# Range tests of five units moved to the end, small copies and weight casts moved to ScalarE, new engine orders

## The chip, the cores and the metric

One core of one Trainium2 chip runs the whole kernel. The metric is the device time of one execution in microseconds (us); the kernel before takes 573.07 us, the median of three runs (572.95 to 573.48).

## The reference, cut to what matters

A gated linear attention with a complex decay runs first; its output goes through one dense layer pair with a Mish-like gate.

```python
# attention: q, k, v, a_re, a_im are (4, 8, 768, 48)
scale = np.minimum(mag, 0.999) / (mag + 1e-06)         # mag = |a|
S_re, S_im = new_re + kv, new_im                       # new = a_n * S, per step t
y[:, :, t] = np.einsum('bhd,bhde->bhe', q[:, :, t], S_re)
# dense part: x is (3072, 384), w_in (384, 2048), w_out (2048, 384)
h = x @ w_in
g = h * np.tanh(np.log1p(np.exp(h)))
out = g @ w_out
```

The inputs of the dense weights arrive as 64-bit words and are turned into fp32 and then into pairs of fp32r parts on the chip.

## The kernel before

**Tiling.** The 3072 tokens are 12 units of 256 (four batches of three units), each of two chunks of 128. A unit passes three stages. `ew_steps(u)` turns the decay into magnitudes and phases (VectorE and ScalarE, tiles of 128 x 768; units 0 and 1 do it in two groups, g0 and g1, of 128 x 384), and ends with four rotations `rot` on VectorE whose results SyncE copies ("relays") into the transposed tile T by small DMAs. `attn_steps(u)` does the attention of two chunks on TensorE (score tile `pa`, transposed keys `pkn`, output `ypsum`, state update `pd`), with masks and state sums on VectorE and copies out of PSUM on ScalarE; its result goes by four DMAs into `xf`, is split into `xH` (ScalarE) and `xL` (VectorE, L258), and these feed the dense part. `moe_steps` has 8 steps a unit: `mm1` (18 matmuls into `ph`, L697, waiting for xH and xL), four ScalarE passes and two VectorE passes over 128 x 512, a split of g into `gh` and `gl`, and `mm2` (12 matmuls into `po`, L734). The first four steps of units 0 and 1 use unsplit weights (L693 and L730).

**The lines that the change touches.** In `test(g)` (L387) VectorE compares R - 0.55 with a quarter of I squared, which `size(g)` left in x3, and sums the result into `good`; the total over `good` decides at the end, behind everything, whether the general path has to run. `grow(g)` ends with two copies of 128 x 6 (L454, L455), on VectorE for units 0 and 1 and on GpSimd for the others. `divide(n)` (L257, L258) casts 16 weight tiles of 128 x 768 and takes the rest: 11 casts on ScalarE, 5 (n = 2, 5, 8, 11, 14) on VectorE. The cast `gh` of steps 1, 3, 5 and 7 is on ScalarE from unit 2 on. `spin` (L522) issues "junk" matmuls of 128 x 512 that compute nothing the output uses: 40 after the first phase (`turned`) and 44 after the first `ypsum` copy.

**What sets the order.** Every step has a place in the plan, in units of dense steps, and a program emits the plan in that order. But the order in which each engine runs its instructions is written out: `ORDER` has a list of instruction numbers per engine (a number is the place at which the plan emits the instruction on that engine, "20+4" stands for 20 to 23), and `in_order` chains the instructions to it. So each of PE, DVE (VectorE), ACT (ScalarE), Pool and SP runs its own list strictly from front to back, and a waiting instruction holds all behind it. SP issues all DMAs.

Of the kernel before, what the change touches and what calls it, by code (L numbers as in the profile page):

```python
# [14 lines left out]
F32 = mybir.dt.float32  # L15
# [12 lines left out]
P = 128  # L28
# [5 lines left out]
NJ = 3  # L34
# [5 lines left out]
HACT, HMOD = 2, 3  # L40
# [8 lines left out]
WREP, WREP2, WK = 40, 44, -9.4  # L49
# [6 lines left out]
KU = 3  # L56
PU = 3
# [64 lines left out]
    """,  # L122
    "DVE": """
# [96 lines left out]
def tile_kernel(ctx, tc, q, k, v, are, aim, w_in, w_out, out):  # L220
# [83 lines left out]
    good = const.tile([P, UNITS + GRP, 3], F32, name="good")  # L304
    ncar = const.tile([P, NJ], F32, name="ncar")
    units = {}

    def ew_steps(u):
        b, uu = divmod(u, NU)
        st = units[u] = {}  # L310
# [681 lines left out]
```

## Time and profile before

| what | value |
|---|---|
| median of three runs | 573.07 us |
| the profiled execution, its time | 572.9 us |
| its span, first to last instruction | 571.2 us |
| TensorE matmul busy | 546.9 us, 96% |
| VectorE busy | 482.8 us, 85% |
| ScalarE busy | 465.0 us, 81% |
| mean granted TensorE clock | 0.995 of full speed |

1.7 us of the profiled time lie outside its span. A row of instructions names line, engine, operation, the tiles out<-in and the shapes; times are us from the start of the span, and a bracket tells how long the engine had been idle and what ended that. A busy TensorE is modelled: matmuls overlap, and the end of one is an estimate. Starts are exact.

### The profile page before, as it was taken

How to read it: one execution, taken by the hardware profiler on the slowest of the kernel's cores; microseconds unless marked ns; L12 is line 12 of the kernel's file. 1: busy time of each engine (PE TensorE's matmuls, PEld its weight loads, DVE VectorE, ACT ScalarE, POOL GpSimd, SP SyncE). 2: the span in 40 equal slices, each digit the busy share in tenths (PEclk: the TensorE clock that was granted, in tenths of full speed). 3: DMA queues.
4: the chain of work that ended last, by engine and by line, in shares of the span. 5: the costliest groups of instructions: out<-in, count | busy, mean ns of one | idle time of the engine just before them, and what ended most of it. 6: DMA issues, size and time to landing. Idle time of an engine off the chain costs nothing.

```text
span 571.2 us, 13311 instructions
## 1 busy us (share of the span) xinstructions
PE 546.9 (96%) x5254; PEld 509.5 (89%) x5254; DVE 482.8 (85%) x865; ACT 465.0 (81%) x749; POOL 39.5 (7%) x55
## 2 busy tenths in 40 slices
PE   0799999999999999999999999999999999999996
PEld 0367877889999999999999999999999999999996
DVE  6999999999999998988988998888897887554543
ACT  7899898999979899798898989679978777446662
POOL 2022322240000000000000000000000000000000
PEclk9899999999999999999999999999999999999999
DMA  8666966805455747606547437316436326201000
GB/s 298 223 200 219 297 204 184 259 16 152 155 151 143 220 127 198 163 16 182 143 143 202 132 91 224 112 43 203 135 93 173 107 75 157 91 22 36 1 29 32
DMA packets 69059, 80.69 MB, mean 141 GB/s; under 512 B 6144, under 2 KB 60672, under 8 KB 68992
## 3 DMA queue, kind: packets, MB, share of 16 engines
q1 hardware_dynamic: 68992, 79.80, 47.2%
q8 instruction: 42, 0.69, 0.5%
q14 instruction: 25, 0.20, 0.1%
HBM read 44.63 MB, written 11.40 MB: 98 GB/s over the span
## 4 chain that ended last, share of the span: by engine, by line
PE 81%; ACT 8%; DVE 6%; DMA 2%; issue 1%; SPq 1%; ACTq 0%; DVEq 0%
PE ph L697 32%; PE po L734 32%; PE ypsum L610 6%; PE pa L583 5%; PE pd L630 2%; PE po L730 2%; ACT L249 2%; DMA T<-QK 1%; PE ph L693 1%; DVE raw L289 1%; ACT R L488 1%; DVE wx L288 1%; PE junk L522 1%; DVE X L425 1%; ACT X L375 1%
## 5 line engine op out<-in xcount | busy, mean ns | idle before, releaser
L697 PE MATMUL ph<-xH,w 128*128 128x256 f32 x1104 | 223.7, 286 | 0.2 <-ACT X L377 0.2
L734 PE MATMUL po<-w,gh 128*128 128x384 f32 x704 | 201.9, 339 | 0.0
L697 PEld LDWEIGHTS ph<-xH,w 128*128 128x128 f32 x1104 | 180.3, 190 | 2.3 <-issue 0.9
L697 PE MATMUL ph<-xL,w 128*128 128x256 f32 x552 | 156.3, 284 | 0.0
L734 PEld LDWEIGHTS po<-w,gh 128*128 128x128 f32 x704 | 128.8, 188 | 2.2 <-issue 1.3
L734 PE MATMUL po<-w,gl 128*128 128x384 f32 x352 | 118.4, 337 | 0.0
L697 PEld LDWEIGHTS ph<-xL,w 128*128 128x128 f32 x552 | 104.7, 190 | 1.2 <-issue 0.8
L701 ACT ACTIVATE e<-ph 128x512 f32<-128x512 f32 (+1 forms) x100 | 57.0, 573 | 43.0 <-PE ph L697 35.5
L707 DVE SCALAR_TENSOR_TENSOR g<-e,ph 128x512 f32<-128x512 f32 (+1 forms) x100 | 65.7, 658 | 20.0 <-ACT e L705 17.2
L703 ACT ACTIVATE e<-e 128x512 f32<-128x512 f32 (+1 forms) x100 | 60.7, 610 | 22.0 <-DVE e L702 21.8
L734 PEld LDWEIGHTS po<-w,gl 128*128 128x128 f32 x352 | 66.2, 188 | 0.2
L702 DVE TENSOR_SCALAR e<-e 128x512 f32<-128x512 f32 (+1 forms) x100 | 40.7, 408 | 27.1 <-ACT e L701 26.9
L258 DVE TENSOR_TENSOR gl<-g,gh 128x512 fp32r<-128x512 f32 x88 | 60.0, 683 | 2.9 <-ACT gh L257 2.5
L705 ACT ACTIVATE e<-e 128x512 f32<-128x512 f32 (+1 forms) x100 | 60.9, 609 | 1.3
L704 ACT ACTIVATE e<-e 128x512 f32<-128x512 f32 (+1 forms) x100 | 60.6, 609 | 1.3
L249 ACT ACT_TABLE_LOAD x43 | 55.2, 1283 | 1.5 <-PEq L948 0.8
L610 PE MATMUL ypsum<-am,V 128*48 128x128 f32 x240 | 36.1, 278 | 0.6 <-DVE am L597 0.6
L522 PE MATMUL junk<-cmask 128*128 128x512 bf16 x84 | 23.1, 419 | 14.1 <-DVE I L431 14.1
L257 ACT CAST gh<-g 128x512 fp32r<-128x512 f32 x40 | 24.5, 612 | 11.9 <-PE po L734 11.1
L291 POOL TENSOR_TENSOR raw<-raw 128x768 int32<-128x768 int32 x16 | 27.4, 1719 | 86.0 <-DVE raw L289 39.3
L610 PE MATMUL ypsum<-T,S 96*48 96x128 f32 x320 | 32.2, 277 | 0.0
L522 PEld LDWEIGHTS <-cmask 128*128 128x128 bf16 x84 | 8.6, 106 | 23.8 <-issue 17.5
(96 smaller groups left out, 841.7 us busy)
## 6 DMA issues: line engine op xcount, KB each, us to landing
T<-X SPq DMA_DIRECT2D x72, 129.0 KB, 2.5
T<-QK SPq DMA_DIRECT2D x72, 129.0 KB, 2.5
raw<-w_in SPq DMA_DIRECT2D x8, 768.0 KB, 7.2
raw<-w_out SPq DMA_DIRECT2D x8, 768.0 KB, 6.9
kd<-vx SPq DMA_DIRECT2D x45, 128.0 KB, 3.0
kn<-kd SPq DMA_DIRECT2D x15, 384.0 KB, 3.7
V<-v SPq DMA_DIRECT2D x12, 384.0 KB, 4.5
out_dram<-o SPq DMA_DIRECT2D x24, 192.0 KB, 2.4
```

What stands on the lines that cost most here:

```text
L249: nc.scalar.preload_act_table_set({"l": "natural_log_exp_and_others", "t": "trig_and_small"}[name])
L258: leng(out=lo, in0=src, in1=h.bitcast(F32), op=ALU.subtract)
L522: ins = nc.tensor.matmul(junk, cmask, cmask.unsqueeze(1).broadcast_to([P, 4, P]), start=True, stop=True)
L610: nc.tensor.matmul(py[64 * par:64 * par + D, i, :], lhs, rhs, start=n == 0, stop=first or n == 1)
L697: nc.tensor.matmul(ph[:, a, :], rows_in(parts[j][:, wp], kt, a), st[xp][:, kt, :], start=n == 0, stop=n == 8)
L701: act(e, ph, AF.Exp)
L702: nc.vector.tensor_scalar_min(e, e, math.exp(20.0))
L703: act(e, e, AF.Square, bias=1.0)
L704: act(e, e, AF.Ln, scale=0.2, bias=0.2)
L705: act(e, e, AF.Exp, scale=-1.0)
L707: nc.vector.scalar_tensor_tensor(g, e, 2.5, ph, ALU.subtract, ALU.mult)
L734: nc.tensor.matmul(po[t], gp[:, a, tsl], rows_out(parts[NPAIR + j][:, wp], a), start=j in starts and a == 0 and n == 0, stop=j + 1 in ends ...
```

## The change

It does four things.

1. `test` of units 0 to 4 (seven VectorE instructions, two each for units 0 and 1) is left out of its old place. `late_steps(u)` loads R and I of these units a second time (ten DMAs of 384 KB, into the same rotating buffers "R" and "I", two each), squares I on ScalarE (five instructions of 128 x 768) and does the seven tests, at places 82 to 89 of the plan's 96.
2. The two small copies of `grow` for units 0 and 1 (eight instructions) go from VectorE to ScalarE.
3. The five weight casts that were on VectorE go to ScalarE (HACT 3), and so do the casts `gh` of unit 1's steps 5 and 7.
4. 50 instead of 40 junk matmuls in the first `spin`, and new lists for all engines.

```diff
-HACT, HMOD = 2, 3
+HACT, HMOD = 3, 3
-WREP, WREP2, WK = 40, 44, -9.4
+WREP, WREP2, WK = 50, 44, -9.4
+LATER, LATE0, LATED = 5, 82, 1.5
...
+    def in_range(out, R, I2, n):
+        nc.vector.scalar_tensor_tensor(out, R, LOW, I2, ALU.subtract, ALU.is_ge, accum_out=good[:, n, 0:1])
+
+    def late_steps(u):
+        st = {}
+
+        def load():
+            for n, src in (("R", are), ("I", aim)):
+                st[n] = io.tile([P, NCH, NJ, C], F32, tag=n, name=n, bufs=RB)
+                nc.sync.dma_start(st[n].rearrange("p c j t -> p (c j) t"), src[u].rearrange("p (a t) -> p a t", t=C))
+
+        def check():
+            R, I = (st[n].rearrange("p c j t -> p c (j t)") for n in "RI")
+            act(I, I, AF.Square, scale=0.5)
+            if u < GRP:
+                for g in range(NCH):
+                    in_range(I[:, g], R[:, g], I[:, g], UNITS + u if g else u)
+            else:
+                in_range(I, R, I, u)
...
-            nc.vector.scalar_tensor_tensor(x3, R, LOW, x3, ALU.subtract, ALU.is_ge, accum_out=good[:, gi(g), 0:1])
+            if u >= LATER:
+                in_range(x3, R, x3, gi(g))
...
-            small = nc.vector if u < 2 else nc.gpsimd
-            small.tensor_copy(QK[..., C:], X[..., C - 1:C])
-            small.tensor_copy(X[..., C:], X[..., C - 1:C])
+            small = nc.scalar.copy if u < 2 else nc.gpsimd.tensor_copy
+            small(QK[..., C:], X[..., C - 1:C])
+            small(X[..., C:], X[..., C - 1:C])
...
-                split(g, gh, gl, nc.scalar.copy if 1 < unit < UNITS and j in GA else nc.vector.tensor_copy, nc.vector.tensor_tensor)
+                split(g, gh, gl, nc.scalar.copy if 0 < unit < UNITS and j in GA else nc.vector.tensor_copy, nc.vector.tensor_tensor)
...
+    for u in range(LATER):
+        load, check = late_steps(u)
+        plan.append((LATE0 + u * LATED, len(plan), load, LATE0 + u * LATED))
+        plan.append((LATE0 + u * LATED + 1, len(plan), check, LATE0 + u * LATED + 1))
```

The lists are long; read against the plan, their fronts say this (first before, then after).

```diff
 "PE"
-        0+20 48+4 40+4 52+4 20+2 56+4 44+4 60+15 22+13 124+4 75+5 128+2 35 132+4 130 188+6 36+2 226+3 38 80+5 136+4 85
+        0+23 58+4 23+5 62+4 50+7 66+8 57 28+21 74+16 134+8 90+5 198+6 95+16 236+6 142+8 111+6 258 150+32 259+5 117 49
 "SP"
-        0+3 8 3 16 5 4 9 17 11 15 18 7 6 20 19 21+3 46 10 12 24 26+2 25 28+2 45 43+2 42 47 13+2 48 51 31 30 35 33+2 32
+        0+2 6 2 8 3 5 4 7 16 9 17 11 15 18 20+2 23 22 19 10 12 46 26 25 24 27 29 28 47 44 42 45 43 14 13 48 51 31+2 30
```

- **SP.** Before, q and k of unit 0's second group (6 and 7) are loaded behind the first relay (18), and five of the six relays of the first group follow them. After, q (6) is the third DMA of all and k (7) the ninth; the six relays (18, 20, 21, 23, 22, 19) follow each other.
- **PE.** Before, 20 junk matmuls stand ahead of the first score tile (48) and 64 between it and the first `mm1` of unit 1 (L697). After, 23 stand ahead of it, 68 between it and that `mm1`, 3 behind; and one more `mm2` step of unit 0 (two instructions of L730, four rows of the trace) stands ahead of it.
- **DVE.** The last rotation of unit 0's first group is number 22 of the list before and 20 after, with the running sum over the phases of the second group now ahead of it; that of unit 0's second group is number 43 and 36, that of unit 1's second group 87 and 74, `xL` of unit 1 131 and 117.
- **ACT.** The arc tangent of unit 0's second group joins that of the first between the same two table loads. Of the instructions ahead of unit 1's `xH`, the eight small copies and one weight cast are new there.
- From the fourth `mm2` of unit 2 on for PE, and from some place in units 3 and 4 on for DVE, ACT and SP, the lists before and after name the same instructions in the same order, but for the late steps. Those lie between the dense steps of unit 10: the late loads behind the last relay of unit 11 on SP (six of them) and behind unit 11's `xf` (four), the squares and tests between the passes of unit 10's steps.

## Rows read from the trace of the kernel before

**Rows 1.** The page: busy time, and TensorE's busy tenths in 40 slices.
```profile
PE 546.9 (96%) x5254; PEld 509.5 (89%) x5254; DVE 482.8 (85%) x865; ACT 465.0 (81%) x749; POOL 39.5 (7%) x55
...
PE   0799999999999999999999999999999999999996
```
**Rows 2.** Busy us by stretch: stretch, length, engines (instructions), PEclk, DMA share, GB/s.
```profile
24.31:30.34 6.03, 5.48 (x35) 4.10 (x35) 5.98 (x14) 4.55 (x9) 0.00 (x0) 0.72 0.88 319
30.34:52.90 22.56, 21.80 (x210) 15.89 (x211) 22.42 (x43) 21.89 (x38) 5.26 (x3) 1.00 0.66 198
52.90:80.80 27.90, 27.82 (x271) 22.23 (x270) 27.86 (x50) 24.69 (x49) 7.51 (x5) 1.00 0.82 253
80.80:136.20 55.40, 55.40 (x416) 47.11 (x415) 54.68 (x84) 51.22 (x81) 17.05 (x12) 1.00 0.49 156
136.20:189.00 52.80, 52.60 (x525) 50.99 (x524) 52.23 (x94) 46.70 (x72) 0.89 (x5) 1.00 0.57 160
...
500.00:525.00 25.00, 25.00 (x242) 24.29 (x234) 13.53 (x28) 13.95 (x25) 0.00 (x0) 1.00 0.12 33
```
**Rows 3.** The same view, the junk matmuls (L522) alone: PE, PEld, PEclk, DMA.
```profile
24.31:80.52 56.21, 15.91 (x64) 6.21 (x64) 0.97 0.76 238
```
**Rows 4.** The chain that ended last, merged: start, us, what.
```profile
75.04 1.35 PE po L730 x4
...
79.36 1.51 PE junk L522 x7
80.87 2.37 PE ph L697 x18
```
**Rows 5.** Timeline at unit 1's entry into the dense part: start, us, instruction.
```profile
79.92 0.96 DVE L258 TENSOR_TENSOR xL<-xf,xH 128x768 fp32r<-128x768 f32 x1
...
80.52 0.47 PE L697 MATMUL ph<-xH,w 128*128 128x256 f32 x1
```
**Rows 6.** Timeline of the first relays and scores, and of unit 1's last rotation.
```profile
16.53 0.55 DVE L387 SCALAR_TENSOR_TENSOR X<-R,X 128x384 f32<-128x384 f32 x1
17.01 0.95 DVE L472 TENSOR_TENSOR QK<-QK,R 128x768 f32<-128x768 f32 x1
19.91 1.84 SPq L468 DMA_DIRECT2D T<-QK  x3
24.31 1.13 PE L595 MATMUL pa<-T 96*128 96x128 f32 x8 [3.40 <-DMA T<-QK]
...
52.05 0.95 DVE L472 TENSOR_TENSOR QK<-QK,R 128x768 f32<-128x768 f32 x1
```
**Rows 7.** First 200 us by form: instruction, count | busy us, mean ns | idle before.
```profile
L387 DVE SCALAR_TENSOR_TENSOR X<-R,X 128x768 f32<-128x768 f32 x4 | 3.8, 948 | 0.0
L257 DVE CAST w<-raw 128x768 fp32r<-128x768 f32 x5 | 2.8, 554 | 0.0
L387 DVE SCALAR_TENSOR_TENSOR X<-R,X 128x384 f32<-128x384 f32 x4 | 2.2, 555 | 0.0
L455 DVE COPY X<-X 128x6 f32<-128x6 f32 x4 | 0.7, 166 | 0.0
...
L257 ACT CAST w<-raw 128x768 fp32r<-128x768 f32 x11 | 10.0, 911 | 0.9 <-DVE w L258 0.8
L552 ACT COPY kn<-pkn 128x384 f32<-128x384 f32 x10 | 4.6, 468 | 1.1 <-PE pkn L551 1.0
L377 ACT ACTIVATE X<-I 128x768 f32<-128x768 f32 x4 | 3.4, 840 | 0.0
L257 ACT CAST gh<-g 128x512 fp32r<-128x512 f32 x4 | 2.5, 616 | 0.8 <-DVE g L707 0.8
L374 ACT ACTIVATION_READ_ACCUMULATOR X<-R 128x1 f32 x6 | 1.1, 190 | 0.0
```
**Rows 8.** DMA issues between 2.33 and 2.6 us: KB, us to landing.
```profile
raw<-w_in SPq DMA_DIRECT2D x1, 768.0 KB, 5.5
```
**Rows 9.** Who waited for whom, ACT from 80.8 to 136.2: total us, times, longest.
```profile
ACT e L703 <- DVE e L702: 2.0, 5, 0.6
```

More of the change, by code (lines that the diff above doesn't have):

```diff
@@ L75 @@
     "PE": """
[46 rows of a table removed]
[46 rows of a table added]
     """,
     "DVE": """
[29 rows of a table removed]
[29 rows of a table added]
     """,
     "Activation": """
[24 rows of a table removed]
[25 rows of a table added]
     """,
     "Pool": """
-        8 3+2 1 5 10 0 7 9 6 2 11 13 12 14+3 18 17 20 19 21+6 29 28 27 31 30 35 33 32 36 34 38 37 40 39 51 41+2 44 43
-        45+2 48 47 49+2
+        8 3+2 1 5 10 0 7 9 6 2 11+6 18 17 20+2 19 22+5 28+5 27 35 34 36 33 38 37 40 39 51 41+2 44 43 45+2 48 47 49+2
     """,
     "SP": """
[13 rows of a table removed]
[13 rows of a table added]
     """,
@@ L306, in tile_kernel @@
     units = {}
+    def in_range(out, R, I2, n):
[14 more added lines that the diff above has]
+                in_range(I, R, I, u)
+        return load, check
     def ew_steps(u):
```

221 rows, old and new, of the table ORDER are left out of this document.

## The prediction

> **What bounds the kernel now.** I read the page first: TensorE is busy for 96% of the span and its slices are full from the third to the last but one [rows 1]. So the end is set by how much TensorE has to do, by what it loses ahead of the full part, and by its tail, and a change that takes nothing off TensorE can gain only where it is not yet full of useful work. The stretches tell where that is. Up to 80.8 us TensorE also looks busy, but from its first score tile at 24.31 [rows 6] to the first `mm1` of unit 1 at 80.52 [rows 5] there are 64 junk matmuls [rows 3], 1.51 / 7 = 0.216 us each [rows 4], 13.8 us in all: filling, in time in which the useful work is not ready. What it waits for is VectorE, busy 27.86 of 27.90 us from 52.9 to 80.8, 54.68 of 55.40 after that and 52.23 of 52.80 up to 189 [rows 2]; ScalarE has 3.2, 4.2 and 6.1 us idle in the same three stretches, much of it waiting for VectorE [rows 9]. The `mm1` at 80.52 starts while `xL` of unit 1, VectorE's instruction from 79.92, still runs [rows 5]: there VectorE sets TensorE's time, and behind it the chain runs through TensorE's dense work without junk [rows 4]. The place to look at is therefore that `mm1`. What TensorE reaches earlier there comes off the end, if ScalarE and VectorE can follow it through the next 110 us.
>
> **What VectorE loses.** Four tests of 128 x 384 at 0.56 and three of 128 x 768 at 0.95 us [rows 7] are 5.1 us. The five weight casts are 5 x 0.55 = 2.8 us [rows 7]. The eight small copies last 0.17 each [rows 7], 1.3 us, but overlap with their neighbours, and I count 0.7. The two `gh` casts I take at 0.4, by the weight cast's 0.55 for half as much again. That makes 9.4 by durations; since an instruction starts some 0.07 us before the one ahead of it ends (16.53 + 0.55 against 17.01 [rows 6]), about 8.5 us, all ahead of 190 us, of VectorE's 98%.
>
> **What ScalarE gets.** Five casts at 0.91 and two `gh` at 0.62 [rows 7] are 5.8 us. A copy of 128 x 6 on ScalarE isn't in the trace; it lies between 0.07 (hidden in its neighbours, as on VectorE) and 0.47, the copy of 128 x 384 [rows 7], and I take 0.2, next to the accumulator read of 0.19 [rows 7], which has as little data: 1.6 us. Sum 7.4 us, of which 1.7 ahead of unit 1's `xH` and the rest up to 150 us, where ScalarE has 4.2 + 3 us idle. The Trainium skill (ScalarE: Activation LUTs, What ACT_TABLE_LOAD costs) gives 186 ns + 0.833 ns per element, less 93 ns overlap; by that a small copy is some 0.1 us, an estimate, and the eight would cost 0.8 rather than 1.6.
>
> **The head, in the new order.** I carried the rows' durations along the new lists, waiting where an instruction needs another's result. (a) q of the second group now comes third on SP. The first weight tile took 5.5 us to land [rows 8] with some 1.3 MB in that time; 192 KB more ahead of it are about 0.5 us. The magnitude of group 0 also loses its test, so the arc tangent comes 0.5 us later, but its first rotation 0.5 earlier, since it no longer stands behind group 1's products. The second rotation, before at 17.01 to 17.97 [rows 6], has the second group's running sum ahead of it and ends at 18.3. (b) SP: before, five relays stood behind two QK loads, and the last one started at 19.91 + 2 x 0.61 = 21.1 [rows 6]. After, three QK relays and one X relay follow the rotation at once: 18.35 + 3 x 0.6 = 20.15. The scores start 1.0 us earlier, at 23.3. (c) Behind that, group 1's rotations end at 28.4 instead of 29.2, and the last rotation of unit 1, before 52.05 to 52.9 [rows 6], ends at 52.2: the arc tangents share a table load, ScalarE pays 0.2 for each small copy, and in the end the sines and cosines of unit 1, ScalarE's, hold VectorE up. Of the 3.4 us that VectorE's list is shorter here, 0.7 arrive. (d) From there to the end of unit 1's `xL` VectorE had 44 instructions in 27.9 us without a gap [rows 2, 5]. Now 43: out are the tests of units 2 and 3, a cast and a carry (2.3 us), in come a state sum, an output row and a minimum that were earlier before (1.1). 1.2 us less; ScalarE has 1.0 more in the same stretch and 3.2 idle. I take half, 0.6, since the copies of `ypsum` and their DMAs ahead of `xL` are a chain of their own; bounds 0 and 1.2. So `mm1` comes 0.7 + 0.6 = 1.3 us earlier, at 79.2 (bounds 0 and 1.9).
>
> **TensorE's list at that point.** One more `mm2` step is done ahead of it: 1.35 us [rows 4] that need not be done later. Three junk matmuls are left behind it, 3 x 0.216 = 0.65 us that weren't there before. The other seven of the ten new ones (three ahead of the scores, four between) lie in waiting time. The list itself, 56.2 us before, grows by 4 x 0.216 + 1.35 = 2.2; from 23.3 on that is 81.7 if all idling in it stays, and the stretch has at least 0.55 + 0.76 us idle and a clock of 0.72 in its first 6.03 us (1.2 GHz for part of it, after 3.4 us without a matmul) [rows 2, 6], 3 us together, which the filling before and behind the scores covers: 78.7, just ahead of the 79.2. Gain: 1.3 + 1.35 - 0.65 = 2.0 us.
>
> **Up to 190 us, and the end.** From 80.8 to 136.2 ScalarE is to do 51.2 + 3.1 = 54.3 us of work in 55.4 [rows 2]: it fits only because VectorE, for which it waited, has 2 us less in the same stretch. I count that as nothing, with the loss below as its rival. From 136 to 189 it is 46.7 + 2.2 in 52.8. Behind that the lists are the same and TensorE is full. The late steps: five squares at 0.84, seven tests, 4.2 and 5.1 us [rows 7], and ten DMAs, around 495 to 530 us, where VectorE is busy 13.5 and ScalarE 13.95 of 25 us and the DMA engines 12% [rows 2]. Their cover is that idle time; each can push a pass of unit 10 back by 0.9 us at most. SP waits with the third pair of loads for the first tests, and `xf` of unit 11 stands behind them; but the mask that `xf` needs is itself behind those tests on VectorE. Zero, bounds 0 and 1 us.
>
> **Sum.** Against the profiled execution: 572.9 - 2.0 = 570.9, with a span of 569.2; it lies 0.17 under the median, so 573.07 - 2.0 = 571.1 us.
>
> **Rivals.** (A) The sum above: 571.1, from 570.0 (all of the 1.9) to 572.3.
> (B) VectorE's whole relief arrives: its list is 4.6 us shorter up to `xL` of unit 1, and if ScalarE doesn't hold it up, `mm1` comes at 75.9 and the time is 573.07 - 4.6 - 0.7 = 567.8. For it speaks VectorE's full stretches, against it that ScalarE is as full from 30 to 53 us, 21.89 of 22.56 [rows 2].
> (C) Nothing arrives: the DMAs in front, the small copies on ScalarE or the junk in TensorE's list eat the 1.3 us, and `mm1` stays at 80.5 or comes at 81.7: 572.4 to 573.6.
> (D) ScalarE becomes the bound, slower. If its idle time of 4.2 us from 80.8 to 136.2 isn't from VectorE's load but from the order of the passes, it stays, and the stretch grows by the 3.1 us; the next one by 2.2. `mm1` of unit 2 has some 1.1 us of slack. 573.07 - 2.0 + 3.1 + 2.2 - 1.1 = 575.3. It decides if ScalarE's idle in 81 to 136 stays above 2 us. For it: only 2.0 us of the 4.2 are waits for `emin` [rows 9], and a weight cast is 0.91 on ScalarE for 0.55 on VectorE [rows 7]. The Trainium skill (ScalarE: Activation LUTs, Rules for kernel authors) says to keep simple arithmetic on VectorE, which is faster per element; these two rows agree.
>
> **How the numbers follow.** A 0.45, B 0.15, C 0.2, D 0.2. 0.2% (1.15 us, to 571.9 and 574.2) is about what a measurement of this kernel can tell from no change. A lies under 571.9 for four fifths, so faster 0.36 + 0.15 + 0.03 of C = 0.54; same 0.09 + 0.15 + 0.02 of D = 0.26; slower 0.2. The range holds A, C, most of B and half of D: 568.3 to 575.0. A's own is 570.0 to 572.3.
>
> **What would show it.** Step (b): the first score tile at 23.3 and the six first relays in one run on SP. (c), (d): unit 1's last L472 ends at 52.2, its first L697 at 79.2 with 68 junk rows between. The next stretch: ScalarE busy 54 of 55 us with under 2 us waited, TensorE without gaps. The late part: no idle on TensorE from 495 to 530. The prediction is wrong if TensorE waits anywhere from 82 to 190, if the first `mm1` of unit 1 isn't earlier, or if SP's late loads hold `xf` of unit 11.

## The result, and the profile after

The changed kernel is **slower**: 576.72 us (575.84 to 577.52) beside 572.89 (572.56 to 573.48) for the kernel before, a ratio of 1.0068 with an interval of 1.0055 to 1.0081. The forecast was 571.1, with a range of 568.3 to 575.0. Two more pairs of measurements on other chips gave 1.0059 (1.0038 to 1.0080) and 1.0044 (1.0029 to 1.0059). The price is therefore 2.5 to 3.9 us; the mean of the three is 1.0057, or 3.3 us.

The page of the changed kernel: busy time of each engine, TensorE's busy tenths in 40 slices, and the shares of the chain that ended last.

```profile
PE 548.6 (95%) x5264; PEld 509.3 (88%) x5264; DVE 481.4 (84%) x850; ACT 472.6 (82%) x769; POOL 38.0 (7%) x55
...
PE   0799999999999999999999999999999999998996
...
PE 64%; ACT 14%; DVE 10%; DMA 6%; SPq 3%; issue 2%; DVEq 0%; ACTq 0%
```

Beside [rows 1], TensorE has 10 more matmuls, all junk, VectorE 15 fewer instructions and ScalarE 20 more. The slices show one dent, an 8 for 518 to 533 us. The others are full, yet TensorE loses time in them too, as the experiments show: a wait of 1 us is hard to see in a slice of 14 us.

Busy time by stretch, in the columns of [rows 2]:

```profile
30.34:52.90 22.56, 22.27 (x209) 15.67 (x206) 21.36 (x38) 22.16 (x41) 3.77 (x2) 1.00 0.67 203
52.90:80.80 27.90, 27.90 (x269) 22.68 (x269) 26.98 (x49) 24.54 (x50) 6.81 (x6) 1.00 0.73 236
80.80:136.20 55.40, 54.93 (x416) 46.97 (x414) 54.13 (x79) 54.06 (x84) 15.54 (x12) 1.00 0.57 175
136.20:189.00 52.80, 52.61 (x524) 50.55 (x523) 50.75 (x88) 47.23 (x74) 1.74 (x4) 1.00 0.53 148
500.00:525.00 25.00, 23.99 (x262) 22.77 (x259) 15.05 (x36) 12.98 (x23) 0.00 (x0) 1.00 0.40 127
```

VectorE is no longer full ahead of 80.8 us, and ScalarE has 1.3 us idle from 80.8 to 136.2 where it had 4.2. That is as the prediction had it.

The timeline of the same kernel: the first score tile, unit 1's first product with q and its last rotation, TensorE's transposition of unit 1's keys (`pkn`), unit 1's `xL`, and its first `mm1` (L721 is L697 of before).

```profile
24.06 1.13 PE L619 MATMUL pa<-T 96*128 96x128 f32 x8 [1.60 <-DMA T<-X]
...
42.72 1.83 DVE L475 TENSOR_TENSOR QK<-QK,X 128x768 f32<-128x768 f32 x2 [0.82 <-DMA QK<-q]
...
51.60 1.43 DVE L496 TENSOR_TENSOR QK<-QK,R 128x768 f32<-128x768 f32 x1
...
52.88 0.52 PE L575 MATMUL pkn<-ident,T 96*128 96x96 f32 x4
...
79.18 0.96 DVE L259 TENSOR_TENSOR xL<-xf,xH 128x768 fp32r<-128x768 f32 x1 [0.69 <-ACT xH L258]
...
80.04 0.59 PE L546 MATMUL junk<-cmask 128*128 128x512 bf16 x2
...
80.28 0.47 PE L721 MATMUL ph<-xH,w 128*128 128x256 f32 x1
```

The first score is 0.25 us earlier than in [rows 6], the last rotation ends where it did (52.05 + 0.95 = 53.0 in [rows 6]), `xL` is 0.74 earlier and `mm1` 0.24 [rows 5].

The late part, in two views. First SP's queue from the `xf` loads of unit 11 on, then ScalarE behind them:

```profile
513.66 0.60 SPq L688 DMA_DIRECT2D xf<-y  x1
...
517.55 0.54 SPq L318 DMA_DIRECT2D R<-a_re  x1
518.13 0.43 SPq L318 DMA_DIRECT2D I<-a_im  x1
```
```profile
519.92 0.62 ACT L727 ACTIVATE e<-e 128x512 f32<-128x512 f32 x1
523.91 0.85 ACT L322 ACTIVATE I<-I 128x768 f32<-128x768 f32 x1 [3.37 <-DMA I<-a_im]
524.67 0.61 ACT L727 ACTIVATE e<-e 128x512 f32<-128x512 f32 x1
525.19 0.61 ACT L728 ACTIVATE e<-e 128x512 f32<-128x512 f32 x1
525.71 0.82 ACT L258 CAST xH<-xf 128x768 fp32r<-128x768 f32 x1
```

The square of unit 3 waits 3.37 us for a load that was issued only at 518.13, behind unit 11's `xf`. The passes of unit 10 and the `xH` of unit 11 stand behind it on ScalarE. In this execution TensorE waits 1.5 us for a `g` and 1.0 for a mask from 490 to 545 us, where before it had no wait.

And the place that the prediction doesn't name at all. VectorE near 256 us, after and before:

```profile
254.79 1.76 DVE L496 TENSOR_TENSOR X<-QK,X 128x1536 f32<-128x1536 f32 x1 [0.22 <-ACT X L512]
257.80 0.69 DVE L731 SCALAR_TENSOR_TENSOR g<-e,ph 128x512 f32<-128x512 f32 x1 [1.25 <-DMA out_dram<-o]
```
```profile
255.09 1.76 DVE L472 TENSOR_TENSOR X<-QK,X 128x1536 f32<-128x1536 f32 x1 [0.22 <-ACT X L488]
256.77 0.68 DVE L707 SCALAR_TENSOR_TENSOR g<-e,ph 128x512 f32<-128x512 f32 x1
```

The order of the instructions here is the same in both kernels. After, `g` waits 1.25 us until an output row has landed, since `g` and the row `o` share three buffers; before, the row had landed. TensorE loses 0.9 us by it: its matmul at 264.82 starts 1.10 us after the one ahead of it, where two such starts are 0.17 apart.

```profile
263.72 0.34 PE L758 MATMUL po<-w,gh 128*128 128x384 f32 x1
264.82 0.36 PE L721 MATMUL ph<-xH,w 128*128 128x256 f32 x1 [0.76 <-DVE g L731]
```

### The profile page after: what moved, and what is told of

Same layout as the page of the kernel before. It is cut to its first block, busy times and chain, and to the rows that moved or that the text cites. A ratio compares the mean times of both kernels' runs of the same rounds, so it can differ in the third digit from the quotient of the medians.

```text
span 575.8 us, 13346 instructions
## 1 busy us (share of the span) xinstructions
PE 548.6 (95%) x5264; PEld 509.3 (88%) x5264; DVE 481.4 (84%) x850; ACT 472.6 (82%) x769; POOL 38.0 (7%) x55
## 4 chain that ended last, share of the span: by engine, by line
PE 64%; ACT 14%; DVE 10%; DMA 6%; SPq 3%; issue 2%; DVEq 0%; ACTq 0%
PE ph L721 24%; PE po L758 23%; PE ypsum L634 6%; PE pa L607 4%; ACT L250 3%; PE pd L654 2%; PE po L754 2%; DMA I<-a_im 2%; DVE g L731 1%; SPq L492 1%; DMA raw<-w_in 1%; ACT e L728 1%; ACT e L725 1%; PE ph L717 1%; PE pa L619 1%
## 5 line engine op out<-in xcount | busy, mean ns | idle before, releaser
L721 PE MATMUL ph<-xH,w 128*128 128x256 f32 x1104 | 223.5, 286 | 2.7 <-DVE g L731 2.7
L721 PEld LDWEIGHTS ph<-xH,w 128*128 128x128 f32 x1104 | 180.2, 190 | 6.4 <-issue 3.5
L721 PE MATMUL ph<-xL,w 128*128 128x256 f32 x552 | 156.0, 283 | 0.2 <-DVE xL L259 0.2
L721 PEld LDWEIGHTS ph<-xL,w 128*128 128x128 f32 x552 | 104.9, 190 | 1.2 <-DVE xL L259 0.5
L546 PE MATMUL junk<-cmask 128*128 128x512 bf16 x94 | 24.7, 406 | 15.2 <-DVE I L455 15.2
L258 ACT CAST gh<-g 128x512 fp32r<-128x512 f32 x42 | 25.7, 611 | 12.9 <-PE po L758 10.7
```

The costliest lines, as they stand in the source:

```text
L546: ins = nc.tensor.matmul(junk, cmask, cmask.unsqueeze(1).broadcast_to([P, 4, P]), start=True, stop=True)
L721: nc.tensor.matmul(ph[:, a, :], rows_in(parts[j][:, wp], kt, a), st[xp][:, kt, :], start=n == 0, stop=n == 8)
```

## The experiments

Theory 1 was that the late part costs the time; theory 2, that the new order and ScalarE's extra work do. Each time below stands beside the kernel before on the same chip, and the ratio is to that. A trace is of one execution, and not always of a middling one: the changed kernel's is the slowest of its six, e2's the fastest of five, e13's the slowest of seven, e14's the slowest of twelve, e15's the fastest of nine. So times are taken from all executions, and traces tell where time goes.

**1. The late part taken out, mended, and alone; the relief alone.** `e1_no_late` has no late steps:

```diff
-    for u in range(LATER):
-        load, check = late_steps(u)
-        plan.append((LATE0 + u * LATED, len(plan), load, LATE0 + u * LATED))
-        plan.append((LATE0 + u * LATED + 1, len(plan), check, LATE0 + u * LATED + 1))
```

> The changed kernel with the late steps left out: range tests of units 0 to 4 are not made at all (their counts are preset), no late loads, no squares. Theory 1 (the late part costs the time, because its squares wait on ScalarE for loads that land late): the three late microseconds are gone, 576.7 - 3.3 = 573.4 us, and TensorE has no idle time between 495 and 530. Theory 2 (the loss is in the new order and in ScalarE's extra work ahead of 490 us): stays at 576 or above. The prediction's own sum, if only the late part was wrong, would be 571.1.

Measured: 575.80 us, 1.0034 (1.0023 to 1.0044). Theory 1 alone would give 573.4. Most of the loss stays with no late step in the program.

`e2_late_sp` changes SP's list alone (374 and 375 are unit 0's late loads, 386 and 387 unit 3's; 382 to 385 are the `xf` loads of unit 11):

```diff
-        345 347+4 344 359+2 351 358 361 354 352 373 372 362+3 357 353 356 368 341 366 365 369+2 367 371 355 374+2
-        378+4 383 376 385 377 384 382 386+4 391 390 392+2
+        345 347+4 344 374+2 359+2 351 358 361 354 352 373 372 362+3 357 353 356 368 341 366 365 369+2 367 371 355
+        378+4 386+2 383 376 385 377 384 382 388+2 391 390 392+2
```

> The changed kernel, with two moves in SP's list alone: the late loads of unit 0 go behind the q load of unit 11 (at about 464 us instead of 491), those of unit 3 ahead of the xf loads of unit 11 (at about 511 instead of 518). All late work stays. Theory 1 (waits of the squares for their data): the waits of 1.5 us at 498 and of 3.4 us at 520 are gone, and what is left, 0.85 us a square, fits the idle time: 573.4 to 573.8 us. Theory 1b (the late work itself, 9.3 us on two engines that feed TensorE, pushes the passes of units 10 and 11 back): only about 1 us less, 575.7.

Measured: 575.79 us, 1.0040 (1.0025 to 1.0054). In its trace no square waits, and TensorE is busy 55.00 of 55.00 us from 490 to 545 (52.48 in the changed kernel's). The waits are mended as planned, and the time is still 2.4 us over the kernel before. That is the 575.7 of theory 1b, but not by its mechanism, since TensorE waits for none of the late work.

`e3_before_late` is the kernel before with the late part alone, `e4_before_notests` the kernel before without the tests of units 0 to 4 and with nothing late. Both have the lists of before, and:

```diff
-HACT, HMOD = 3, 3
+HACT, HMOD = 2, 3
-WREP, WREP2, WK = 50, 44, -9.4
+WREP, WREP2, WK = 40, 44, -9.4
```

> The kernel before with the late part alone: tests of units 0 to 4 out of their places and the late loads, squares and tests at the end as in the changed kernel; order, casts, small copies and junk matmuls of before. Theory 1: 572.9 + 3.3 = 576.2, less what the tests' absence gives in the head (0 to 1.1 us): 575.1 to 576.2. Theory 2 (new order and ScalarE's extra work are the cause): 572 to 573.

> The kernel before with the range tests of units 0 to 4 left out (counts preset) and nothing late: only VectorE's relief of 5.1 us by durations, in the order of before. If VectorE sets the time of unit 1's first mm1 (the prediction's step d), it comes 0.7 to 1.5 us earlier than 80.5 and the time is 571.4 to 572.2. Rival: TensorE's own list up to there (useful work and junk) is as long, so that the relief doesn't reach it: mm1 at 80.2 to 80.5 and 572.6 to 572.9.

Measured: 575.26 us, 1.0030 (1.0020 to 1.0041), and 572.75, 0.9986 (0.9977 to 0.9995). So the late part costs 2.5 us in the order of before, and the relief of 5.1 us on VectorE brings 0.8 there. In e4 `mm1` comes at 80.89, though `xL` starts 0.2 us earlier than before: the relief doesn't move that place at all, as the rival had it. Neither theory is enough by itself: e4 and e1 have the same tests and no late part, and lie 3 us apart.

**2. Ten junk matmuls.** The traces of the changed kernel, e1 and e2 have the wait of `g` at 256 us in common; those of before, e3 and e4 don't have it. What differs there is not the order of the work but the fetch of TensorE's code. The program has 42 blocks of 16 KB (0.69 MB) on an instruction queue of their own. TensorE's 10528 instructions (5264 matmuls and as many weight loads) are 251 for each block; VectorE, the next, has 850 in all, so these are TensorE's blocks. One view of each kernel's DMAs around that output row, after and before (queues, packets, share; then the issues with KB and us to landing):

```profile
q1 hardware_dynamic: 135, 0.18, 22.4%
q8 instruction: 1, 0.02, 3.0%
issues: line engine op xcount, KB each, median us to landing
out_dram<-o SPq DMA_DIRECT2D x1, 192.0 KB, 3.4
```
```profile
q1 hardware_dynamic: 144, 0.20, 29.2%
issues: line engine op xcount, KB each, median us to landing
out_dram<-o SPq DMA_DIRECT2D x1, 192.0 KB, 1.8
```

After, a block is fetched from 255.43 to 256.49 as one packet of 16384 bytes; 120 of the row's 128 packets are done by 255.75, and the last eight, a sixteenth of the row, start one by one from 256.48 on and end at 257.23. Before, the row is through at 256.05 and the block comes at 256.37. The Trainium skill (Runtime: NRT & Kernel Launch, Instruction fetch mechanics) says that code is refilled in 16 KiB blocks of 256 instructions and that crossing a block's boundary is mostly hidden. The size agrees with the 42 blocks; hidden it is for TensorE itself, which in the kernel before has one wait of over 0.15 us from 82 us on (0.2, for ScalarE), but not for the row that it meets. The Trainium skill (DMA: Bandwidth & Descriptors, Queues, rings and completion order) says that a DMA engine takes turns between queues by whole packets, which agrees with the eight packets that come after the block's 1.06 us.

Theory C: ten more matmuls in the list move all later fetches ahead against the work, into the output rows. Three kernels test it, with the changed kernel again beside them.

> The changed kernel again, beside the next three. If the late part's cost is what its trace shows (3.2 us of TensorE's time, of which the two moves of SP's loads give back nearly all), it is 2 to 3 us above the kernel with the two moves. Theory C (a 16 KB block of TensorE's code, fetched at 255.4 us, holds the last packets of an output row, for whose buffer VectorE's g waits): TensorE's gap of 0.9 us at 264.8 is there again, and the row issued at 254 lands 3.4 us or more after its issue. Rival (a landing that varies by chance): the gap is there in some executions only.

`e6_before_junk50`:

```diff
-WREP, WREP2, WK = 40, 44, -9.4
+WREP, WREP2, WK = 50, 44, -9.4
...
-        0+20 48+4 40+4 52+4 20+2 56+4 44+4 60+15 22+13 124+4 75+5 128+2 35 132+4 130 188+6 36+2 226+3 38 80+5 136+4 85
+        0+30 58+4 50+4 62+4 30+2 66+4 54+4 70+15 32+13 134+4 85+5 138+2 45 142+4 140 198+6 46+2 236+3 48 90+5 146+4 95
```

> The kernel before with nothing but 10 more junk matmuls in the first run, ahead of the first score tile, where TensorE waits anyway: no useful work, order or engine is changed. Theory C: ten more matmuls in TensorE's code move each later block's fetch ahead by some 1.2 us against the work, so that the fetch meets the output row at 254 us: landing 3.4 us or more instead of 1.8, a gap of 0.9 us on TensorE near 265, and 573.7 to 574.6 us beside 573.1 (0.6 to 1.2 slower). Rival (the gap comes from the new order of the work): landing stays 1.8, no gap, within 0.3 of before.

`e7_sp_junk40` is e2 with

```diff
-WREP, WREP2, WK = 50, 44, -9.4
+WREP, WREP2, WK = 43, 41, -9.4
```

> The changed kernel with the two moves of the late loads, and with 10 junk matmuls fewer (3 of 23, 4 of 21 and 3 of 16 in three runs that fill waiting time): TensorE's code has as many instructions as before. Theory C: the row at 254 us lands 1.8 us after its issue, the gap at 265 is gone, 0.9 us faster than 575.8 of the kernel with the two moves. Rival (order): the gap stays and the time too. If the junk matmuls were needed for the clock, the head loses 0.3 us or more.

Measured: the changed kernel 577.03 (1.0059), the kernel before with ten more junk matmuls **575.76, 1.0040** (1.0028 to 1.0052), the changed kernel with ten fewer and the SP moves **573.56, 1.0004** (0.9996 to 1.0013). Theory C has the direction right and the size too small: 2.6 us (2.3 by the ratio) where 0.6 to 1.2 were expected of e6, and 2.1 (against e2, by the ratios) where 0.9 was expected of e7. Nothing in e6 is reordered, and the traces place its loss: the same useful matmul starts 0.4 us later than in the kernel before at 83 us (the first score, at 24.73, waits for its relay), 0.8 at 230 and 2.7 at 275, and it stays at 2.7 to the end. The 0.4 in between goes with the row issued at 208 us, for whose buffer VectorE's `o` waits 1.0 us, the 1.9 with the row issued at 255. Its VectorE at the same place, and TensorE behind it:

```profile
255.93 1.76 DVE L472 TENSOR_TENSOR X<-QK,X 128x1536 f32<-128x1536 f32 x1 [0.22 <-ACT X L488]
259.81 0.69 DVE L707 SCALAR_TENSOR_TENSOR g<-e,ph 128x512 f32<-128x512 f32 x1 [2.12 <-DMA out_dram<-o]
```
```profile
265.57 0.34 PE L734 MATMUL po<-w,gh 128*128 128x384 f32 x1
266.84 0.36 PE L697 MATMUL ph<-xH,w 128*128 128x256 f32 x1 [0.93 <-DVE g L707]
```

And e7's VectorE:

```profile
254.67 1.76 DVE L496 TENSOR_TENSOR X<-QK,X 128x1536 f32<-128x1536 f32 x1 [0.22 <-ACT X L512]
256.35 0.68 DVE L731 SCALAR_TENSOR_TENSOR g<-e,ph 128x512 f32<-128x512 f32 x1
```

Two more kernels close the circle. `e9_after_junk40` is the changed kernel with e7's line and nothing else, `e12_before_junk30` the kernel before with ten junk matmuls fewer.

> The changed kernel with nothing but the 10 junk matmuls taken out (3 of 23, 4 of 21 and 3 of 16 in three runs); late part as in the change. Theory C (code blocks meeting output rows cost 2.2 us): 577.0 - 2.2 = 574.8, rows at 208 and 254 us land in under 2.1 us. What it lies above the 573.6 of the same kernel with the two moves on SP is the late part's price without any meeting: 1.2 by the timed runs so far, up to 3.2 by the changed kernel's trace. If the ten junk matmuls aren't the cause: 577.

> The kernel before with 10 junk matmuls fewer (30 of the first kind and 41 of the second less, as 3 of 20, 4 of 13 and 3 of 14). Theory C (a block's fetch costs only where it meets a row that is waited for): 572.9 to 573.5, fetches near 208 and 254 us begin 1.8 us or more behind the row's issue. Rival (each junk matmul costs time by itself, 2.6 us for ten, whatever it meets): 570.6.

Measured: 573.31, 1.0007 (0.9995 to 1.0019), and 573.15, 1.0003 (0.9994 to 1.0012). Ten junk matmuls out of the changed kernel give 2.9 us back; out of the kernel before they give nothing. So it isn't a price for each matmul. In e12's trace the useful matmuls start 0.4 us later than before at 85 us and from 142 us to the end: a later head, and no loss behind it. Worked out from the traces' packets, for the two output rows that are issued near 208 and 254 us (us from the row's issue):

```text
kernel                fetch begins   row lands    fetch begins   row lands
                      (row at 208)                (row at 254)
before                 3.9            1.8          1.8            1.8
e12, ten fewer         4.3            1.9          4.3            1.8
e9,  after less ten    1.5            1.8          1.6            1.8
e7                     1.9            1.9          1.8            1.8
after                  1.6            2.0          1.2            3.4
e5,  after again       1.1            4.1          1.1            4.2
e6,  before plus ten   1.3            4.3          1.4            4.3
e2                     1.0            4.1          1.2            3.5
```

For these two rows, in all 18 traces, a fetch that begins 0.98 to 1.46 us after the issue goes with a landing of 3.4 to 4.4 us (15 rows), one that begins at 1.49 or later with 1.8 to 2.0 (21 rows). A third row, near 390 us, lands 3.9 to 4.5 us after its issue in six traces, all of the new order with 50 junk matmuls, and 2.2 to 2.4 in the others; in two of the six (e1, e14) the fetch began as late as 1.9 and 2.2. The packets tie all 21 late landings to the block: each time the same share of the row, eight of 128 packets, is missing when the other 120 are through, and it starts within 0.02 us of the block's end, in e1 and e14 too. Why those eight stand still already before the block's recorded begin stays open. A late landing alone proves nothing: in the kernel before, the rows issued at 196 and 351 us take 3.5 and 3.6 us and meet no block.

So the changed kernel has two losses behind its head. Against e9's trace, its useful matmuls fall back by 1.5, 3.7 and 3.1 us at the three rows in its three traced executions (after, e5, e13), and by 2.7, nothing and 1.8 us from 490 to 545 us, in the late part.

**3. The head, the late part and the casts.** `e8_sp_aim` is e2 with the `a_im` load of unit 2 issued at 23.6 us instead of 33.0, `e10_before_late_sp` is e3 with e2's two moves, `e11_all_moves` is e7 with e8's move and two changes in VectorE's list (of numbers; here by what they name):

```diff
     VectorE, near 166 us
-    u4 turn, u2 step 3 g
+    u2 step 3 g, u4 turn
     VectorE, near 126 us
-    u0 step 6 gh, u1 step 3 o, u1 step 3 o
+    u1 step 3 o, u1 step 3 o, u0 step 6 gh
```

> The changed kernel with the two moves of the late loads and one more on SP: the a_im load of unit 2 goes from 33.0 us to 23.6, behind the a_re load, where SP is idle. Theory H (the relief of VectorE in the head is lost at unit 1's first grow, which waits 0.6 to 1.3 us for q of unit 1 to land): q is issued 0.6 earlier, with 384 KB less ahead of it, and lands 1 us or more earlier; the wait is gone, unit 1's xL and its first mm1 come 0.5 to 0.8 earlier, and the time is 575.0 to 575.3. Rival: the relays of unit 0's second group wait behind the 384 KB instead, and nothing is gained or 0.5 lost.

> The kernel before (its order, casts, copies and 40 junk matmuls) with the late part of the change and the two moves of late loads on SP. If the squares' waits for their data are all that the late part costs: as the kernel before without the tests, 572.75, plus at most 0.5: 572.7 to 573.3, against 575.3 without the two moves. If the late work itself (9.3 us on VectorE and ScalarE) costs: 574 or more.

> The changed kernel with every repair so far: 10 junk matmuls fewer, the two moves of the late loads, the a_im load of unit 2 earlier on SP, and two changes of VectorE's order (g of unit 2's fourth step ahead of unit 4's turn at 168 us; the two output rows of unit 1's first half ahead of a gh cast at 126). Expected from the traces: 573.56 - 0.5 (q of unit 1 lands in time) - 0.4 - 0.4 (TensorE's gaps at 127.5 and 169.6 us) = 572.3. If the head's half microsecond is given back further on, as in the change: 573.

Measured: e8 575.30, 1.0038 (1.0024 to 1.0053); e10 573.20, 1.0003 (0.9994 to 1.0012); e11 **572.08, 0.9980** (0.9971 to 0.9989). In e8's trace the wait for q is gone, and `mm1` comes at 79.27, but the time is within its interval of e2's: inconclusive. Its trace loses 3.3 us at the three rows against e7's. By the ratios e10 lies 1.0 us over e4 and e3 2.5: of the late part's price in the order of before, 1.5 us are the waits for the loads, and up to 1.0 is the late work itself. In their traces that work costs TensorE nothing: e10's useful matmuls start within 0.1 us of e4's from 200 us to the end.

`e13_after_third` is the changed kernel and `e14_late_sp_second` is e2, both again; `e15_dve_moves` is e11 without e8's move; `e16_all_casts_dve` is e11 with five weight casts and two `gh` casts back on VectorE:

```diff
-HACT, HMOD = 3, 3
+HACT, HMOD = 2, 3
...
-nc.scalar.copy if 0 < unit < UNITS and j in GA else nc.vector.tensor_copy
+nc.scalar.copy if 1 < unit < UNITS and j in GA else nc.vector.tensor_copy
```

> The changed kernel a third time, beside the next one on the same chip, for the price of the late part as it stands. Theory: 1 to 3 us above the kernel with the two moves of the late loads (by its traces 0.5 to 3.2, since the loads land 4 to 6.4 us after their issue). Rival: as in the pair without the ten junk matmuls (573.3 and 573.6), no difference.

> The changed kernel with the two moves of the late loads, a second time, beside the changed kernel itself. No square waits for its data; TensorE loses nothing from 490 to 545. 1 to 3 us faster than the changed kernel beside it, if those waits are what the late part costs.

> The kernel with all the repairs, without the earlier a_im load of unit 2: so 10 junk matmuls fewer, the two moves of the late loads and the two changes of VectorE's order. If VectorE's order gave most of the 1.5 us between 573.56 and 572.08: 572.1 to 572.8. If the a_im load's place (q of unit 1 in time) gave most: 573.0 to 573.5.

> The kernel with all the repairs (572.08), with the five weight casts and unit 1's two gh casts back on VectorE, each just ahead of the subtraction that needs it; the small copies stay on ScalarE. The prediction's premise (VectorE sets TensorE's time up to 190 us, so that 3.6 us more on VectorE cost): unit 1's first mm1 0.5 to 1.2 later, and 572.6 to 573.3. Rival D (ScalarE is the bound after the move, and 5.8 us less on it help): 571.5 or less. If neither engine sets the time there: 572.1.

Measured: e13 576.35, 1.0044 (1.0029 to 1.0059); e14 575.99, 1.0042 (1.0031 to 1.0054); e15 **571.94, 0.9975** (0.9965 to 0.9985); e16 576.53, 1.0057 (1.0041 to 1.0073). e11 and e15 are faster than both kernels, e15 by 1.4 us than the kernel before. Without e8's move e15 is no slower than e11, so q's landing gave nothing that can be measured. By the ratios e7 lies 1.7 us over e15; TensorE's two losses at VectorE's two places are 0.8 us of that, by the starts of its matmuls, and since e15's traced head is also 0.8 us ahead of e7's, the rest isn't shown to be theirs. e13 and e14 differ by 0.4 us, which isn't measurable, although TensorE loses 1.8 us near 505 and 530 us in the one traced execution of e13. The price of the late part as it stands is thus between nothing (e13 and e14; e9 and e7) and 2.5 us (e3 and e4). In the traces it goes with the landing of the `a_im` loads of units 0 and 3, 4.1 and 4.4 us after their issue in e9, 5.1 and 3.9 in e5, 5.4 and 5.3 in e13, 6.4 and 5.8 in the changed kernel; why that varies stays open.

TensorE's waits from 80 to 190 us in e16 (who waited for whom, us in total, times, longest):

```profile
PE po L754 <- DVE g L731: 1.3, 1, 1.3
PE pa L607 <- DVE S L659: 0.7, 1, 0.7
PE ph L721 <- DVE g L731: 0.6, 2, 0.4
PE po L758 <- DVE o L771: 0.5, 1, 0.5
```

Each ends with VectorE; e15 has 0.7 us of waits there. All three expectations for e16 (571.5 to 573.3) were too low. The casts were put just ahead of the instruction that needs them, and another place might cost less, so the 4.4 us between e16 and e11 are the price of the casts in these places.

## Why the prediction was wrong

**What bounds the kernel.** Right that TensorE is full from 81 us on and that all depends on what it loses. Wrong about the place chosen: the `mm1` at 80.52 starts beside `xL`, but a lighter VectorE doesn't move it. In the twelve traced executions with the new order `mm1` starts 55.6 to 57.4 us after the first score tile; before it is 56.2, in e4, with VectorE relieved, 56.35. From TensorE's transposition of unit 1's keys, at 51.4 to 55.4 us, `mm1` follows after 27.3 to 27.9 us in all 18 executions: there TensorE's own list sets the time. Ahead of that it doesn't, since seven junk matmuls fewer make the stretch no shorter (28.8 us from the first score in the changed kernel, 29.0 in e9, which waits 1.5 us more). The prediction had computed that list at 78.7, "just ahead of the 79.2", and taken the other side of a difference of 0.5 us.

**Step (a), (b).** The first score was forecast at 23.3 and came at 24.06. The six relays do stand in one run, but from 17.03 on, with the last at 21.29 (forecast 20.15): the first rotation ended 0.4 us later instead of 0.5 earlier, and the second at 19.39 instead of 18.3. A part is in the sum itself: by the prediction's 1.3 MB in 5.5 us, the 192 KB of q are 0.8 us and not 0.5. Over the twelve executions the score comes between 23.5 and 25.3 us, so a gain of 1.0 was at the edge of what the loads' landing makes of it.

**Step (c).** The last rotation was forecast to end at 52.2 and ended at 53.02. Behind the 0.8 us are the wait for q in the timeline above, a load that the prediction followed for unit 0 but not for unit 1, and the rotation itself, which lasted 1.43 us where it was 0.95 before; why it did stays open. In e15, where the wait is 0.2 and the rotation 0.95, it ends at 51.98. The 0.7 that "arrive" were counted from 52.9, while [rows 6] has the end at 53.0.

**Step (d) and TensorE's list.** `mm1` at 79.2 was forecast and 80.28 measured; 68 junk matmuls lie between, as forecast. In e15, the best head, with 61, it is 79.26. The arithmetic of the head, then, describes its good executions; its middle one is `mm1` at 80.3. The other term, 1.35 - 0.65 = 0.7 us less behind `mm1`, fits e11 and e15, 490.0 us from `mm1` to the end of the span where the kernel before has 490.7, but e4 has 489.6 without that move, so it isn't shown by itself; e9 has 491.1, the changed kernel 495.5.

**Junk in waiting time.** This is the step that failed: "The other seven of the ten new ones ... lie in waiting time", costed at nothing. They do cost no time where they stand. But they are ten more matmuls of code, and ten of them are worth 2.1 (e2 against e7) to 2.9 us (the changed kernel against e9, a pair whose traces also differ in the late part); in e6's trace all but 0.4 us of its loss is paid behind 208 us, where code blocks met output rows. No rival had this mechanism; C and D named the junk and ScalarE in their own stretches only.

**Up to 190 us.** ScalarE was to be busy 54 of 55 us and is, 54.06; it waits 0.8. Rival D's price is near the measured time, but that is luck: ScalarE's load there costs nothing that shows, and taking the casts back cost 4.4 us where e16 put them (against e11). The small copies last 0.19 us (186 to 200 ns), where 0.2 was taken, but the next instruction starts 0.09 to 0.10 us after the start of seven of the eight, so that they cost the 0.1 us of the prediction's other figure. And "TensorE without gaps" was wrong by some 0.4 us each, by the starts of its matmuls, at 127.5 and 169.6, the two places of VectorE's list that e11 and e15 mend: there output rows stood behind a `gh` cast of 1.69 us (0.76 in e11), and a `g` behind `turn`. The kernels with both mended lie 1.4 (e11) and 1.7 us (e15) under e7.

**The late part.** The prediction said zero, with bounds of 0 and 1 us, and that "the mask that `xf` needs is itself behind those tests". It looked at who waits for SP and not at what SP's order does to the loads behind `xf`, nor at landing: [rows 8] had a load of twice this size land after 5.5 us, and a square placed one step behind its load waits for that. The size was 0 to 2.5 us by the times, and up to 2.7 in a trace.

**The sum that the runs give**, as ratios by 573.1 us: e15, with all the overlooked places mended, is at -1.4 where the forecast had -2.0. Without the mending of VectorE's two places it is +0.2 (e7), with the late part as it stands +0.4 (e9), and with ten more junk matmuls +3.3, the changed kernel. "What would make it wrong" listed waits of TensorE from 82 to 190, `mm1` not earlier, and SP's late loads holding `xf`. The first is so, with 0.7 us; the second is nearly so; the third isn't: `xf` held the loads.

## What to carry to other kernels

Instructions that fill waiting time are not free because the engine waits there. Here they shifted the fetches of code, which go by the count of instructions, and were paid for some 200 us later. When a kernel's time moves at places where nothing was changed, compare the landing times of the same transfers in both traces, and look for the queue of code among the DMAs; then change the count of filler alone, on the old kernel too.

Work that is moved into idle time needs its data there. On an engine that runs its list in order, a wait for a load holds all that stands behind it (3.4 us on ScalarE at 520 us, of which TensorE lost 1.5), so count a late load from its place in the issuing queue and with a measured landing time.

## What the runs showed of the hardware

A fetch of one code block is one packet of 16384 bytes, 1.06 us long in the changed kernel at 255 us and 1.54 in e6. Of the two 192 KB rows that are issued near 208 and 254 us in each of the 18 traces, the 15 whose fetch began 0.98 to 1.46 us after the issue landed in 3.4 to 4.4 us, the 21 whose fetch began from 1.49 on in 1.8 to 2.0. In each late one a sixteenth of the row, eight packets, starts only when the block has ended. Ten matmuls more in the kernel before moved the fetch near 208 us from 3.9 to 1.3 us behind the row's issue, and the one near 254 from 1.8 to 1.4.
